# Linear attention and a token mixer on one core: PSUM tiles, transposes of x, the denominators' constant and the order of all steps are changed

## The chip, the core and the metric

The kernel runs on one core of one Trainium2 chip. The time is device microseconds, lower is better. A core has five engines with queues of their own that run side by side and in order: PE (TensorE, products of matrices; its loads of weights overlap with its products), DVE (VectorE), ACT (ScalarE), POOL (GpSimd) and SP (SyncE, which issues the transfers here). PE writes to PSUM, which has eight banks of 2 KB in each of 128 partitions; DVE and ACT read it from there, POOL works in SBUF.

## The reference, cut to what matters

Inputs are q, k and v of shape (8 batches, 8 heads, 576 positions, 64), and three weights. The attention has no softmax:

```
phi(x)  = [relu(x) * cos(theta * pos), relu(x) * sin(theta * pos)]     # 128 features
kv      = sum over positions of phi(k) outer v                         # 128 x 64 per head
z       = sum over positions of phi(k)
num     = phi(q) @ kv
den     = phi(q) @ z + 1e-06
x       = num / den, heads side by side                                # (8, 576, 512)
```

The mixer then works on x of each batch, with d_hyper = 64:

```
W     = (x @ w_q) @ (x @ w_k).T / 8
out   = relu(W @ x) @ w_out                                            # (8, 576, 512) float32
```

## The kernel before, in words

Loads and stores are float32, all products are in bfloat16 with float32 sums. The work is cut into half batches H = 0 to 15 (four heads each) and batches b = 0 to 7. A string, `ORDER`, lists some 500 steps; the program goes through it and issues each step's instructions, so on every engine's queue the instructions stand in that order. `KE3@A` is step KE of H = 3 on ACT (`@V` DVE, `@G` POOL); the digit behind a colon is a PSUM tile, or for OE one of ten output buffers. What the steps do, with their lines:

- `LQ`, `LK`, `LV` (line 130): SP loads q, k or v of H, in two transfers, into one of four raw buffers; the fifth load waits until the first buffer was read. `LW` loads the weights.
- `RQ`, `RK` (198 to 202), `CV`: relu or cast of a raw buffer to bfloat16, on POOL or ACT, into one of two buffers.
- `VS` (208): DVE multiplies v by the cosine and sine tables. The tables' two spare columns make the sums z come along as a 65th column.
- `KV` (221): 36 products give kv and z. `KE` (234) copies them to SBUF.
- `QT` (230): 18 transposes of 64 rows bring q's positions to the free axis. `QM` (238) multiplies them by the tables on DVE, for both halves of the features.
- `N` (254), one for each half of H's heads, g = 0 to 31: 20 products give numerators and, in the 65th column, denominators for ten groups of positions. Two small products (260) of a tile of ones and a tile `eps_t` add 1e-06 to the denominators in PSUM; `eps_t` holds the constant as the sum of two bfloat16 numbers, in two rows.
- `X` (268, 269): DVE takes the reciprocal of ten denominators per partition and multiplies the numerators by it, into x.
- `XT` (285): ten transposes of 128 by 128 turn x of H round, `XE` copies the result to xT (helper lines 189 on ACT, 193 on DVE).
- `WK` (302), `WQ` (315), `KX` (328): x @ w_k, x @ w_q, and the product of the first with x, which takes the place of the large matrix W. `KW`, `QW`, `XK` copy their results to SBUF.
- `MX` (339), `ME` (350, 352): the mixed rows, i = 0 to 31, and their scaled relu.
- `WO` (359), `OE`, `ST` (369): the last product for 36 tiles of 128 rows, its copy to one of ten output buffers, and SP's store.

PSUM is cut into five tiles. `PQ` (two banks) is used by QT and KV alone, each in a part of its own. Two tiles of two banks take N, XT and MX in turn, as the digits 1 and 2 in `ORDER` say. Two tiles of one bank (3 and 4) take WK, WQ, KX and WO. A product into a tile waits until what was in it has been read.

SP's queue holds the loads and the stores in the order of the list: a store that waits for its OE holds up the loads behind it.

Of the kernel before, what the change touches and what calls it, by code (L numbers as in the profile page):

```python
# [12 lines left out]
FP32 = mybir.dt.float32  # L13
# [6 lines left out]
EPS_HI = 9.9837780e-07  # L20
# [4 lines left out]
LQ0 LQ1 TB0 RQ0@G QT0 RQ1@G LV0 LV1 LK0 QM0 LW0 CV1@G LK1 CV0@A LV2 LQ2 VS0 RQ2@G QT1 LV3 QM1  # L25
RK0@A KV0 LK2 RK1@A VS1 CV3@G LQ3 LK3 KE0@V LW1 N1:1 X1 CV2@A LQ4 KV1 VS2 KE1@A N0:2 X0 CW0@A
N2:1 LV4 RK2@G LV5 RK3@G X2 QT2 QM2 XT0:2 LK4 N3:1 RQ4@G X3 XE0@A CV4@G KV2 KE2@A LQ5 LK5 N4:2
VS3 XT1:1 RQ3@A QT3 XE1@A CW1@A KV3 N5:1 X4 QM3 LW2 KE3@A LV6 RK4@G WK0:30 KW0@A WQ0:40 LQ6 N7:2
X5 QT4 N6:1 X7 KX0:30 XT2:2 X6 XK0@A XT3:1 XE2@A VS4 KV4 CV5@G LK6 LQ7 QW0@A MX2:2 LV7 XE3@V
ME2@A MX3:1 LK7 ME3@A LV8 WQ1:30 MX0:2 WK1:40 ME0@A KE4@V MX1:1 LQ8 QW1@A QM4 N8:2 ME1@A RQ5@G  # L30
QT5 KW1@A VS5 RK5@G N9:1 CW5@A KV5 X8 CW3@A X9 CW2@A LK8 CW4@A KX1:30 XK1@A XT4:2 XE4@A KE5@V
LV9 WO1:40 WO2:30 QM5 N11:2 OE1:0@A LQ9 CV6@G VS6 OE2:1@A N10:1 WO3:40 RQ6@G X11 QT6 RK6@A LK9
X10 LV10 RQ7@G MX7:2 LQ11 ME7@A OE3:2@A WO0:30 QM6 XT5:1 XE5@V MX5:2 ME5@V QT7 OE0:3@A KV6 KE6@A
WQ2:40 N12:1 CV7@G VS7 QW2@A MX4:2 ME4@A WK2:30 RK7@G LK11 LQ10 CV8@G KV7 KW2@A X12 N13:2 QM7
RQ8@G ST0 MX6:1 KX2:30 ME6@A LK10 X13 WO5:40 KE7@A XK2@A VS8 WO4:30 N15:1 QT8 RK8@G N14:2 X15
OE5:4@A X14 OE4:5@A KV8 KE8@A LV11 WO6:40 RQ9@G OE6:6@A XT6:1 XT7:2 WO8:30 XE6@A QM8 MX8:1 ME8@A
XE7@V MX9:2 ME9@A WQ3:40 CV9@G ST2 VS9 QT9 N17:1 MX10:2 RK9@G KV9 CV10@G LQ12 LV12 OE8:7@A
ME10@A WK3:30 MX11:2 X17 QM9 N16:1 QW3@A WO7:40 KW3@A KE9@A KX3:30 X16 VS10 ME11@A RQ10@A N18:1
X18 LK12 N19:2 X19 ST1 QT10 XK3@A ST4 WO10:30 LQ13 OE7:8@A WO12:40 RQ11@G OE12:9@A ST3 QM10
XT9:1 XT8:2 XE8@V RK10@G KV10 XE9@A CV11@G QT11 QM11 MX15:1 OE10:3@A RK11@G CV12@G MX12:2 WQ4:40  # L40
QW4@A WK4:30 WO11:40 RK12@G LK13 ME15@A ME12@V KW4@A VS11 VS12 MX13:2 RQ13@G MX14:1 KE10@A
ME13@A KX4:30 KV11 RQ12@A ME14@A XK4@A N21:2 OE11:1@A ST11 QT12 N20:1 KE11@A WO13:30 X21 X20
OE13:0@A LV13 KV12 ST7 LQ14 MX16:2 ME16@A N22:1 QM12 WO14:40 WO16:30 OE14:5@A ST14 LV15 X22
RK13@G KE12@A OE16:2@A N23:2 X23 QT13 MX19:1 ST5 WO9:40 ME19@A OE9:1@A QM13 XT11:2 XE11@A CV13@G
LV14 XT10:1 XE10@V WO17:30 OE17:8@A WO15:40 N25:2 LQ15 MX17:1 ME17@A VS13 RQ14@G X25 KV13 WK5:30
KE13@A N27:1 MX18:2 ME18@A OE15:5@V WQ5:40 ST6 QT14 X27 QW5@A ST16 KW5@A LK14 N24:2 X24 N26:1
X26 LK15 CV15@G QM14 WO21:40 KX5:30 RQ15@A ST15 XT13:2 XK5@A OE21:4@A XE13@V ST17 XT12:1 WO20:30
CV14@G XE12@A VS14 RK14@G ST13 OE20:6@V WO18:40 MX20:2 ME20@V ST9 MX23:1 ME23@A KV14 WQ6:30
KE14@A N28:1 QW6@A ST10 QT15 VS15 MX22:2 ME22@A RK15@G ST20 X28 WK6:30 KV15 KW6@A QM15 KE15@V
MX21:2 N29:1 OE18:2@A KX6:30 ME21@A X29 WO25:40 OE25:5@V N31:2 XK6@A X31 N30:1 X30 WO23:30  # L50
OE23:8@A ST23 WO24:40 XT14:2 XT15:1 OE24:0@A XE15@V ST18 WO22:40 XE14@A ST25 MX25:2 MX24:1
ME24@V WK7:30 OE22:1@A ME25@A KW7@A WQ7:40 QW7@V MX26:1 MX27:2 ME27@V WO26:30 OE26:3@A ME26@V
KX7:40 XK7@V ST12 WO27:30 OE27:6@A ST26 ST8 MX28:2 ME28@A MX31:1 ST22 ME31@V WO30:40 OE30:8@A
MX29:1 MX30:2 WO29:30 OE29:2@A ME29@V ST21 ST30 WO19:40 ST27 ST29 OE19:5@A ST19 WO28:30 OE28:9@A
ME30@V ST24 ST28 WO34:40 OE34:3@A ST34 WO35:30 OE35:7@A WO31:40 ST35 OE31:1@A ST31 WO32:30
OE32:4@V ST32 WO33:40 OE33:8@A ST33
# [4 lines left out]
def kernel(  # L61
# [15 lines left out]
    P = 128  # L77
# [38 lines left out]
    PQ = psum.tile([P, 2, 2048], U8, name="ps_qk")  # L116
    PT = [PQ] + [psum.tile([P, 2, 2048], U8, name=f"ps_p{i}") for i in range(2)]
# [27 lines left out]
    ones_t = pool.tile([P, P], BF16, name="ones")  # L145
    eps_t = pool.tile([P, SC], BF16, name="eps")
# [7 lines left out]
    def tables():  # L154
# [15 lines left out]
        nc.gpsimd.memset(ones_t, 1.0)  # L170
        nc.gpsimd.memset(eps_t, 0.0)
        for p in (0, H2):
            nc.gpsimd.memset(eps_t[p:p + 1, :], EPS_HI)
            nc.gpsimd.memset(eps_t[p + 32:p + 33, :], 1.0e-6 - EPS_HI)
# [37 lines left out]

    qt_v = PQ[:, :, 0:2 * S].bitcast(BF16)
    kv_v = PQ[:, :, 2 * S:2 * S + 4 * 2 * (D + 1)].bitcast(FP32)

    def KV(H, ps, eng):
        for c in range(C):
            for pr, r in ((0, 0), (1, 1), (1, 0), (0, 1)):
                a = slice(H2 * r, H2 * r + H2)
                o = slice(H2 * pr, H2 * pr + H2)  # L220
                nc.tensor.matmul(  # L221
                    kv_v[o, r, :], rk_b[H % NPREP][a, pr, c, :],
                    v2_b[H % NV2][a, pr, c, :, 0:D + 1],
                    start=(c == 0), stop=(c == C - 1))
# [209 lines left out]
```

## Time and profile before

| | |
|---|---|
| median of 3 runs | 126.11 us (125.97 to 126.49) |
| profiled execution | 127.19 us |
| its span, first to last instruction | 125.1 us |
| granted clock of PE over the span | 0.995 |
| PE busy | 102.2 us (82%), 2200 products |
| DVE busy | 92.4 us (74%), 123 instructions |
| ACT busy | 74.8 us (60%), 120 instructions |
| POOL busy | 55.2 us (44%), 59 instructions |
| read from and written to HBM | 29.62 MB and 9.44 MB, 312 GB/s over the span |

The span leaves out what lies before the first and behind the last instruction. Busy time is the time in which an engine had an instruction in work; on PE the ends are modelled, so a busy PE is not a PE at its peak, and overlapping instructions make durations longer than the distance from one start to the next. The view of 40 slices gives the busy share of an engine in tenths, a digit for 3.1 us. In the view of waits a line names the engine that waited, what it waited for, the total in us, how often, and the longest. In a timeline each line has the start in us, the duration in us, engine, line, operation and shapes.

### The profile page before, as it was taken

What the parts mean: (1) busy time and instruction counts of PE and PEld (TensorE: products, weight loads), DVE (VectorE), ACT (ScalarE), POOL (GpSimd) and SP (SyncE); (2) the same over time, 40 slices, a digit from 0 to 9 for tenths busy, and PEclk for the clock granted to TensorE, in tenths of its full rate; (3) what the DMA queues carried; (4) which work ended last, traced back from release to release, by engine and by line L of the source; (5) the groups of instructions that cost most, each with busy time, mean ns of one, the idle gap of its engine ahead of it and who ended that gap; (6) DMA issues with size and microseconds to landing.
All of it is one profiled execution on the core that took longest, in us unless ns stands there. A gap on an engine that the chain in (4) does not pass through costs nothing.

```text
span 125.1 us, 5077 instructions
## 1 busy us (share of the span) xinstructions
PE 102.2 (82%) x2200; PEld 66.7 (53%) x2200; DVE 92.4 (74%) x123; ACT 74.8 (60%) x120; POOL 55.2 (44%) x59
## 2 busy tenths in 40 slices
PE   0120768899696999899997999999997999999980
PEld 0110656787564556657654756575752756643430
DVE  1049598748996999899898698989698879576020
ACT  7523643443688784665874779686637673926640
POOL 7736067364947398696397263034332700000000
PEclk9999999999999999999999999999999999999998
DMA  4999999999999999999999910799999700808994
GB/s 113 337 383 374 391 397 367 378 391 390 387 393 390 391 389 390 389 378 396 398 399 399 362 56 0 194 303 375 392 403 387 279 19 0 335 34 313 371 375 170
DMA packets 20613, 39.38 MB, mean 315 GB/s; under 512 B 3184, under 2 KB 3184, under 8 KB 20592
## 3 DMA queue, kind: packets, MB, share of 16 engines
q1 hardware_dynamic: 20592, 39.07, 85.0%
q8 instruction: 17, 0.28, 0.9%
q14 instruction: 4, 0.03, 0.1%
HBM read 29.62 MB, written 9.44 MB: 312 GB/s over the span
## 4 chain that ended last, share of the span: by engine, by line
PE 57%; DMA 20%; DVE 6%; issue 4%; SPq 4%; POOL 3%; ACT 3%; POOLq 0%; ACTq 0%
PE ps_s L359 19%; DMA kraw<-in_k_dram 10%; PE ps_qk L221 8%; PE ps_p L254 7%; PE ps_s L328 6%; DMA out_dram<-o 5%; PE ps_p L285 5%; DMA qraw<-in_q_dram 5%; PE ps_s L302 4%; SPq L130 3%; PE ps_p L339 3%; PE ps_s L315 3%; PE ps_qk L230 3%; DVE x L269 3%; POOL rk L185 2%
## 5 line engine op out<-in xcount | busy, mean ns | idle before, releaser
L359 PE MATMUL ps_s<-wow,mix 128*128 128x512 bf16 x144 | 34.8, 380 | 0.7 <-ACT kx L189 0.7
L238 DVE TENSOR_TENSOR qm<-ps_qk,qtab 128x2304 bf16<-128x2304 bf16 x16 | 21.6, 1352 | 8.5 <-PE ps_qk L230 5.3
L269 DVE TENSOR_TENSOR x<-ps_p,rec 128x640 bf16<-128x640 f32 x32 | 26.4, 824 | 1.1
L189 ACT COPY o<-ps_s 128x512 f32<-128x512 f32 x32 | 18.7, 588 | 13.8 <-PE ps_s L359 13.5
L208 DVE TENSOR_TENSOR v<-vb,vtab 128x2304 bf16<-128x2304 bf16 x16 | 23.6, 1483 | 1.8 <-ACT vb L189 1.8
L185 POOL TENSOR_SCALAR rk<-kraw 128x1152 bf16<-128x1152 f32 x13 | 18.8, 1444 | 13.9 <-DMA kraw<-in_k_dram 7.9
L191 POOL TENSOR_SCALAR vb<-vraw 128x1152 bf16<-128x1152 f32 x14 | 17.3, 1239 | 14.0 <-DMA vraw<-in_v_dram 7.2
L185 POOL TENSOR_SCALAR rq<-qraw 128x1152 bf16<-128x1152 f32 x12 | 15.7, 1308 | 15.6 <-DMA qraw<-in_q_dram 12.1
L359 PEld LDWEIGHTS <-mix 128*128 128x128 bf16 x144 | 12.8, 98 | 14.7 <-issue 1.5
L254 PE MATMUL ps_p<-kvs,qm 64*128 64x65 bf16 x640 | 16.5, 200 | 3.2 <-issue 2.1
L350 ACT ACTIVATE mix<-ps_p 128x576 bf16<-128x576 f32 x23 | 14.7, 652 | 6.1 <-PE ps_p L339 6.0
L221 PE MATMUL ps_qk<-v,rk 64*64 64x130 bf16 x576 | 13.4, 242 | 5.6 <-ACT rk L183 4.0
L254 PEld LDWEIGHTS <-qm 64*128 64x128 bf16 x640 | 13.6, 100 | 8.0 <-issue 7.6
L230 PE MATMUL ps_qk<-ident,rq 64*128 64x64 bf16 x288 | 8.0, 202 | 9.0 <-POOL rq L185 8.6
L221 PEld LDWEIGHTS <-rk 64*64 64x64 bf16 x576 | 10.6, 120 | 7.9 <-ACT rk L183 4.1
L189 ACT COPY xT<-ps_p 128x1280 bf16<-128x1280 bf16 x9 | 11.0, 1227 | 4.5 <-PE ps_p L285 4.5
L285 PE MATMUL ps_p<-ident,x 128*128 128x128 bf16 x160 | 11.8, 231 | 0.4 <-issue 0.4
L285 PEld LDWEIGHTS <-x 128*128 128x128 bf16 x160 | 10.3, 103 | 2.8 <-DVE x L269 0.9
L230 PEld LDWEIGHTS <-rq 64*128 64x128 bf16 x288 | 6.1, 101 | 10.8 <-POOL rq L185 8.9
L268 DVE RECIPROCAL rec<-ps_p 128x10 f32<-128x10 f32 x32 | 6.9, 215 | 6.3 <-PE ps_p L260 5.8
L328 PE MATMUL ps_s<-x,wk 128*128 128x512 bf16 x40 | 10.0, 381 | 0.0
L189 ACT CAST kvs<-ps_qk 128x260 bf16<-128x260 f32 x12 | 4.6, 384 | 6.9 <-PE ps_qk L221 4.4
(44 smaller groups left out, 96.0 us busy)
## 6 DMA issues: line engine op xcount, KB each, us to landing
qraw<-in_q_dram SPq DMA_DIRECT2D x32, 288.0 KB, 6.0
vraw<-in_v_dram SPq DMA_DIRECT2D x32, 288.0 KB, 5.9
kraw<-in_k_dram SPq DMA_DIRECT2D x32, 288.0 KB, 6.0
out_dram<-o SPq DMA_DIRECT2D x36, 256.0 KB, 2.7
wof<-in_moe_w_out_dram SPq DMA_DIRECT2D x1, 1024.0 KB, 8.1
wqf<-in_moe_w_q_dram SPq DMA_DIRECT2D x1, 128.0 KB, 6.3
wkf<-in_moe_w_k_dram SPq DMA_DIRECT2D x1, 128.0 KB, 6.7
```

The costliest lines, as they stand in the source:

```text
L185: eng.tensor_scalar(dst, s, FMAX, 0.0, op0=ALU.min, op1=ALU.max)
L189: A.copy(dst, s)
L191: G.tensor_scalar(dst, s, 1.0, 1.0, op0=ALU.mult, op1=ALU.mult)
L208: V.tensor_mul(v2_b[H % NV2][:, :, :, :, 0:D], vb_b[H % NPREP].unsqueeze(3).to_broadcast([P, 2, C, 2, D]), vtab.unsqueeze(1).to_broadcast( ...
L221: nc.tensor.matmul(kv_v[o, r, :], rk_b[H % NPREP][a, pr, c, :], v2_b[H % NV2][a, pr, c, :, 0:D + 1], start=(c == 0), stop=(c == C - 1))
L230: nc.tensor.transpose(qt_v[:, r, c * H2:(c + 1) * H2], rq_b[H % NPREP][a, c, :, :], ident[a, a])
L238: V.tensor_mul(qm_b[H % NQM][:, :, :, 0:C, :].rearrange("p s r c d -> p s r (c d)"), qt_v.unsqueeze(1).to_broadcast([P, 2, 2, S]), qtab.re ...
L254: nc.tensor.matmul(nv[:, pr, u, :], qm_b[H % NQM][a, s, r, 2 * u:2 * u + 2, :], kv_b[H % 2][a, r, s, 0:D + 1], start=(u == 0 and s == 0), ...
L269: V.tensor_tensor(x_b[b % NX][:, :, 4 * h:4 * h + 4, :].rearrange("p u (w r) d -> p r w u d", r=2)[:, r], nv[:, :, :, 0:D], rec.to_broadca ...
L285: nc.tensor.transpose(o[:, w, u * P:(u + 1) * P], x_b[b % NX][:, u, hd:hd + 2, :], ident)
L328: nc.tensor.matmul(o, wk_b[b % 2][:, u, :, :], x_b[b % NX][:, u, :, :], start=(u == 0), stop=(u == SC - 1))
L359: nc.tensor.matmul(o, mix_b[bp % 2][:, m, rt * P:(rt + 1) * P], wow[:, m, :], start=(m == 0), stop=(m == NDM - 1))
```

## The change

Five things are changed together.

- PSUM: `PQ` is gone. There are three tiles of two banks, 0, 1 and 2, and QT and KV take whichever of them the list names, as N, XT and MX do.
- The constant: the products of `ones_t` and `eps_t` and both tiles with their memsets are gone. X starts with an instruction on DVE that adds 1e-06 to the ten denominators and writes them to SBUF; the reciprocal then works on that buffer in place.
- XT: twenty transposes of 64 rows instead of ten of 128, the two halves of the positions into one bank each. XE reads both banks and writes xT in the layout it had.
- Engines: on DVE 3 of the XE (before 7), 6 of the ME (9), 2 of the KE (4), no XK (1) and 8 of the OE (4); the others of these are on ACT. POOL has 13 RQ, 14 RK and 15 CV (before 12, 13 and 14).
- Order: the whole list is new. The first loads were q0, q1, v0, v1, k0 and are now q0, v0, k0, v1, k1, q1. Stores stand behind other loads.

```diff
-EPS_HI = 9.9837780e-07
...
-LQ0 LQ1 TB0 RQ0@G QT0 RQ1@G LV0 LV1 LK0 QM0 LW0 CV1@G LK1 CV0@A LV2 LQ2 VS0 RQ2@G QT1 LV3 QM1
-RK0@A KV0 LK2 RK1@A VS1 CV3@G LQ3 LK3 KE0@V LW1 N1:1 X1 CV2@A LQ4 KV1 VS2 KE1@A N0:2 X0 CW0@A
...
-QW4@A WK4:30 WO11:40 RK12@G LK13 ME15@A ME12@V KW4@A VS11 VS12 MX13:2 RQ13@G MX14:1 KE10@A
-ME13@A KX4:30 KV11 RQ12@A ME14@A XK4@A N21:2 OE11:1@A ST11 QT12 N20:1 KE11@A WO13:30 X21 X20
...
-ME30@V ST24 ST28 WO34:40 OE34:3@A ST34 WO35:30 OE35:7@A WO31:40 ST35 OE31:1@A ST31 WO32:30
-OE32:4@V ST32 WO33:40 OE33:8@A ST33
+LQ0 LV0 TB0 RQ0@G QT0:2 QM0 CV0@G LK0 RK0@A VS0 KV0:2 KE0@A N0:0 N1:1 LV1 LK1 RK1@A CV1@G VS1
+LQ1 RQ1@G LV2 LQ2 X1 X0 KV1:2 KE1@A CV2@G LK2 RK2@G RQ2@A QT1:2 QM1 N2:2 QT2:1 XT0:0 VS2 QM2 LQ3
+RQ3@G LV3 X2 CV3@G LK3 RK3@G XE0@A LW1 N3:0 LV5 LQ4 RQ4@G LK4 KV2:1 KE2@A QT3:2 N5:1 X3 XT1:0
...
+ME5@A RK7@G N13:2 KV7:1 KW2@A KX2:40 LQ8 OE2:2@A KE7@A XK2@A RQ7@G QT7:1 LQ9 CV8@G LK8 RQ9@G LV9
...
+OE11:6@V KW4@A CV12@G KV11:1 KE11@A WQ4:30 QW4@A N22:0 X22 N23:2 MX15:1 LV13 KX4:40 CV13@G ST11
...
+WQ5:30 N26:0 ST10 ST15 QW5@A VS14 XT12:1 N27:2 OE16:4@A X26 XE12@A ST0 WO18:30 WO20:40 OE20:8@A
+LQ15 RQ14@G QT14:0 MX22:1 OE18:9@A ST18 X27 XT13:2 XE13@V KV14:0 WO21:40 ME22@A WO9:30 OE21:7@A
...
+ST26 KE15@A N31:1 N30:2 XK6@A MX24:0 ME24@A X31 WO19:30 OE19:4@A WO24:40 OE24:0@A WO25:30 XT14:0
+XE14@A X30 XT15:1 OE25:3@V ST25 ST21 ST13 ST8 ST19 MX26:2 WO22:40 XE15@V MX25:1 MX27:0 OE22:9@V
+ME25@A ME27@V WQ7:30 QW7@A WK7:40 WO23:30 KW7@A KX7:40 OE23:3@A ST22 ST20 ST9 ST24 ST17 ST23
+ME26@V WO29:30 OE29:7@V XK7@A MX31:1 MX29:0 MX30:2 WO27:40 WO30:30 ME31@V MX28:1 ME30@V OE27:6@A
+ME29@A OE30:5@V ST30 ST29 ST27 ME28@A WO28:40 OE28:4@A ST28 WO35:30 OE35:9@A WO34:40 ST35
+OE34:8@A ST34 WO31:30 WO33:40 OE31:1@A ST31 OE33:0@V ST33 WO32:30 OE32:2@A ST32
...
 
...
     mix_b = bufs(2, [P, NDM, 2 * S], BF16, "mix")
     o_b = bufs(NOUT, [P, DM], FP32, "o")
 
-    PQ = psum.tile([P, 2, 2048], U8, name="ps_qk")
-    PT = [PQ] + [psum.tile([P, 2, 2048], U8, name=f"ps_p{i}") for i in range(2)]
+    PT = [psum.tile([P, 2, 2048], U8, name=f"ps_p{i}") for i in range(3)]
     PT += [psum.tile([P, 2048], U8, name=f"ps_s{i}") for i in range(2)]
     place = {}
 
...
     vtab = pool.tile([P, C, 2, D], BF16, name="vtab")
     qtab = pool.tile([P, 2, C, H2], BF16, name="qtab")
     ident = pool.tile([P, P], BF16, name="ident")
-    ones_t = pool.tile([P, P], BF16, name="ones")
-    eps_t = pool.tile([P, SC], BF16, name="eps")
     wq_f = pool.tile([P, NDM, DH], FP32, name="wqf")
     wk_f = pool.tile([P, NDM, DH], FP32, name="wkf")
     wo_f = pool.tile([P, NDM, DM], FP32, name="wof")
...
                 nc.scalar.activation(b[:, pr, :, :, D:DV],
                                      ki.unsqueeze(3).to_broadcast([P, C, 2, 2]),
                                      AF.Sin, bias=0.0, scale=coef)
-        nc.gpsimd.memset(ones_t, 1.0)
-        nc.gpsimd.memset(eps_t, 0.0)
-        for p in (0, H2):
-            nc.gpsimd.memset(eps_t[p:p + 1, :], EPS_HI)
-            nc.gpsimd.memset(eps_t[p + 32:p + 33, :], 1.0e-6 - EPS_HI)
         for b in qm_b:
             nc.gpsimd.memset(b[:, :, :, C, :], 0.0)
 
...
             vb_b[H % NPREP].unsqueeze(3).to_broadcast([P, 2, C, 2, D]),
             vtab.unsqueeze(1).to_broadcast([P, 2, C, 2, D]))
 
-    qt_v = PQ[:, :, 0:2 * S].bitcast(BF16)
-    kv_v = PQ[:, :, 2 * S:2 * S + 4 * 2 * (D + 1)].bitcast(FP32)
+    def qt_view(H):
+        return PT[place["QK", H]][:, :, 0:2 * S].bitcast(BF16)
+
+    def kv_view(H):
+        return PT[place["QK", H]][:, :, 2 * S:2 * S + 4 * 2 * (D + 1)].bitcast(FP32)
 
     def KV(H, ps, eng):
+        place["QK", H] = ps[0]
+        kv_v = kv_view(H)
         for c in range(C):
             for pr, r in ((0, 0), (1, 1), (1, 0), (0, 1)):
                 a = slice(H2 * r, H2 * r + H2)
...
                     start=(c == 0), stop=(c == C - 1))
 
     def QT(H, ps, eng):
+        place["QK", H] = ps[0]
+        qt_v = qt_view(H)
         for c in range(C):
             for r in range(2):
                 a = slice(H2 * r, H2 * r + H2)
...
 
     def KE(H, ps, eng):
         cast(eng, kv_b[H % 2][:, :, :, 0:D + 1],
-             kv_v.rearrange("p r (s e) -> p r s e", s=2))
+             kv_view(H).rearrange("p r (s e) -> p r s e", s=2))
 
     def QM(H, ps, eng):
         V.tensor_mul(
             qm_b[H % NQM][:, :, :, 0:C, :].rearrange("p s r c d -> p s r (c d)"),
-            qt_v.unsqueeze(1).to_broadcast([P, 2, 2, S]),
+            qt_view(H).unsqueeze(1).to_broadcast([P, 2, 2, S]),
             qtab.rearrange("p s c d -> p s (c d)").unsqueeze(2).to_broadcast([P, 2, 2, S]))
 
     def num(t):
...
                     nc.tensor.matmul(
                         nv[:, pr, u, :], qm_b[H % NQM][a, s, r, 2 * u:2 * u + 2, :],
                         kv_b[H % 2][a, r, s, 0:D + 1],
-                        start=(u == 0 and s == 0), stop=False)
-        for pr in range(2):
-            a = slice(H2 * pr, H2 * pr + H2)
-            nc.tensor.matmul(nv[:, pr, :, D], ones_t[a, :], eps_t[a, :],
-                             start=False, stop=True)
+                        start=(u == 0 and s == 0), stop=(u == SC - 1 and s == 1))
 
     def X(g, ps, eng):
         H, r = divmod(g, 2)
         b, h = divmod(H, 2)
         rec = rec_b[g % 3]
         nv = num(place["N", g])
-        V.reciprocal(rec, nv[:, :, :, D:D + 1])
+        V.tensor_scalar_add(rec, nv[:, :, :, D:D + 1], 1.0e-6)
+        V.reciprocal(rec, rec)
         V.tensor_tensor(
             x_b[b % NX][:, :, 4 * h:4 * h + 4, :].rearrange(
                 "p u (w r) d -> p r w u d", r=2)[:, r],
             nv[:, :, :, 0:D], rec.to_broadcast([P, 2, SC, D]), op=ALU.mult)
 
     def xt_view(i):
-        return PT[i].rearrange("p t e -> p (t e)").bitcast(BF16)[:, 0:2 * SC * P].rearrange(
-            "p (w n) -> p w n", w=2)
+        return PT[i].bitcast(BF16)[:, :, 0:2 * SC * H2].rearrange(
+            "p t (w u d) -> p t w u d", w=2, u=SC)
 
     def XT(H, ps, eng):
         b, h = divmod(H, 2)
         place["XT", H] = ps[0]
         o = xt_view(ps[0])
-        for w in range(2):
-            for u in range(SC):
-                hd = 4 * h + 2 * w
-                nc.tensor.transpose(o[:, w, u * P:(u + 1) * P], x_b[b % NX][:, u, hd:hd + 2, :],
-                                    ident)
+        for u in range(SC):
+            for w in range(2):
+                for t in range(2):
+                    a = slice(H2 * t, H2 * t + H2)
+                    hd = 4 * h + 2 * w
+                    nc.tensor.transpose(o[:, t, w, u, :], x_b[b % NX][a, u, hd:hd + 2, :],
+                                        ident[a, a])
 
     def XE(H, ps, eng):
         b, h = divmod(H, 2)
-        dst = xT_b[b % NXT][:, 2 * h:2 * h + 2].rearrange("p w c d -> p w (c d)")
-        cast(eng, dst, xt_view(place["XT", H]))
+        dst = xT_b[b % NXT][:, 2 * h:2 * h + 2].rearrange("p w (u t) d -> p w t u d", t=2)
+        cast(eng, dst, xt_view(place["XT", H]).rearrange("p t w u d -> p w t u d"))
 
     def bank(ps):
         t = PT[ps[0]]
```

## The prediction

> **What bounds the kernel now.** I read the page's busy shares first, then the row of slices, the chain that ended last, the waits, and the DVE and PE timelines. No engine is full: PE 82%, DVE 74%, ACT 60%. The slices and the chain are these.
>
> ```profile
> PE   0120768899696999899997999999997999999980
> DVE  1049598748996999899898698989698879576020
> DMA  4999999999999999999999910799999700808994
> ...
> PE 57%; DMA 20%; DVE 6%; issue 4%; SPq 4%; POOL 3%; ACT 3%; POOLq 0%; ACTq 0%
> ```
>
> PE and DVE are both high in nearly every slice from 15 to 106 us; the DMA engines have a hole at 71 to 78 us and one near 100. The chain is mostly PE, so PE looks like the bound. The waits say that it is a pair:
>
> ```profile
> DVE rec L268 <- PE ps_p L260: 5.8, 11, 0.9
> DVE qm L238 <- PE ps_qk L230: 5.3, 2, 5.1
> DVE qm L238 <- PE ps_qk L221: 2.0, 2, 1.8
> DVE xT L193 <- PE ps_p L285: 2.0, 3, 1.0
> SPq L369 <- ACT o L189: 17.1, 11, 8.9
> ```
>
> DVE waits for products of PE in short pieces; SP stood up to 8.9 us at a store whose rows ACT had not written (that is the first hole). DVE's timeline gives the price of an instruction, as the distance from start to start of neighbours that wait for nothing:
>
> ```profile
> 44.35 0.21 DVE L268 RECIPROCAL rec<-ps_p 128x10 f32<-128x10 f32 x1
> 44.59 0.82 DVE L269 TENSOR_TENSOR x<-ps_p,rec 128x640 bf16<-128x640 f32 x1
> 45.33 0.21 DVE L268 RECIPROCAL rec<-ps_p 128x10 f32<-128x10 f32 x1
> 45.58 0.82 DVE L269 TENSOR_TENSOR x<-ps_p,rec 128x640 bf16<-128x640 f32 x1
> 46.32 1.35 DVE L238 TENSOR_TENSOR qm<-ps_qk,qtab 128x2304 bf16<-128x2304 bf16 x1
> 47.58 0.81 DVE L193 COPY xT<-ps_p 128x1280 bf16<-128x1280 bf16 x1
> ```
>
> The division of 10 sums holds the engine 0.245 us, the product behind it 0.74, a QM 1.27, an XE 0.73. Read in the same way: VS 1.27, ME on DVE 0.68, OE 0.61, KE 0.34; on ACT XE 1.14, ME 0.56, OE 0.50, KE 0.30, a relu or cast of a raw buffer 1.07. On PE the timeline gives these:
>
> ```profile
> 57.81 1.28 PE L285 MATMUL ps_p<-ident,x 128*128 128x128 bf16 x20
> 58.93 1.03 PE L359 MATMUL ps_s<-wow,mix 128*128 128x512 bf16 x4
> ...
> 60.97 0.44 PE L230 MATMUL ps_qk<-ident,rq 64*128 64x64 bf16 x18
> 61.24 0.47 PE L254 MATMUL ps_p<-kvs,qm 64*128 64x65 bf16 x20
> 61.55 0.17 PE L260 MATMUL ps_p<-eps,ones 64*128 64x5 bf16 x2
> 61.58 0.28 PE L339 MATMUL ps_p<-wq,kx 64*128 64x288 bf16 x2
> ```
>
> Twenty 128-row transposes (two XT) take 1.12 us, 18 transposes of 64 rows (a QT) 0.27, the pair with the constant 0.03. A WO takes 0.88 (32 matmuls in 7.04 at the end), KV 0.65, N without the pair 0.30, KX 1.09, WK 0.69, WQ 0.61, MX 0.17. The rest goes by its group's mean less 0.1 (ACT), or as it stands (POOL: q 1.31, k 1.44, v 1.24).
>
> **The change part by part.**
>
> Constant on PE removed: 32 pairs by 0.03 is 1.0 us of PE. Six small memsets on POOL (3.09 to 3.95 us) go too; POOL's first relu of q starts at 4.50 behind them, but q0 was issued at 0.74 and the quickest q load took 2.9 us, so at most 0.8 us is to be had; I take 0.
>
> Constant on DVE added: 32 adds of 10 elements from PSUM, each read by the reciprocal behind it. The row nearest is the reciprocal, also 10 elements from PSUM and also read by the next: 0.245 us each, 7.8 us in all. The reciprocal now reads SBUF and waits for the add; no row shows that. Low end: 0.14 us, what the chain counts for a reciprocal, 4.5 us in all. High end: 0.26, 8.3. I take 7.8. [...]
>
> Transposes: 20 of 64 rows at QT's rate are 0.30 us; with some switching I put 0.35 against 0.56, so 16 XT save 3.4 us of PE. If the halves didn't overlap, nothing; at QT's rate exactly, 4.2. XE reads the same 1280 elements, in runs of 64 from two banks: ACT at the same price; DVE at the same (3 of them), at worst double, 2.2 us more.
>
> PSUM tiles: QT and KV leave their own tile and share three with N, XT and MX: 112 uses over three, where it was 80 over two and 32 over one. PE work between two uses of a tile has a median of 1.8 us now and 1.7 before; in 20 cases of 109 it is shorter than the reader's own time, before in 22. I take no gain and no loss; a bound either way is the wait of DVE for ps_qk named above, 2 us.
>
> Order and engines. DVE gives away four XE, three ME, two KE and one XK, and takes four OE: 3.9 us less, so with the adds 4.0 more. ACT gets four XE, three ME, two KE, one XK, loses four OE and three raw casts: 2.1 more; the three casts go to POOL, 4.0 more. PE has 4.3 less.
>
> To see where these fall I added the prices along each order's list, engine by engine, in four stages of eight X steps (DVE, PE, ACT, POOL, us). Before: 18.5 10.7 10.1 13.3; 22.2 19.4 16.0 14.5; 21.6 23.4 18.2 16.1; 19.9 19.7 12.1 7.9. After: 20.1 7.5 7.2 15.8; 22.4 21.4 22.9 17.4; 21.8 21.0 15.2 14.7; 21.8 22.6 16.1 8.0. What is left for PE behind the last X: 17.1 before, 13.5 after. So the saving on PE turns up behind the last X, where DVE is idle, and up to it PE has nearly the same (72.5 against 73.2), DVE 3.9 more, ACT 4.9 more.
>
> Start. Loads land 1.5 us apart (casts start at 6.99, 8.49, 10.06, 11.59). With the new order v0 is the second, k0 the third: k0 at 8.5 and not 11.6. From there: RK0 to 9.6, KV0 (1.19 in these early microseconds) to 10.8, KE0, N0 and N1 to 12.6, X1 and X0 to 15.1. But q1 is now the sixth load: 13.1, so QM1 ends at 16.4, VS2 17.7, QM2 19.3, X2 20.5. At 20.5 DVE then has 74.7 us listed up to its last X; before, at 20.9, 71.2. The early start is given back to the late q1.
>
> PE runs at half pace until 28.3 us (the 20 products of an N last 0.73 before and 0.48 after it), though the granted clock reads 0.9 or more. [...] PE may warm some microseconds sooner or later; DVE leads there, so I put 0, bounds 1 us either way.
>
> Middle. Before, DVE took from 20.9 to 106.1 for 71.2 us of work, so 13.9 were waits. With the same waits the last X ends at 20.5 + 74.7 + 13.9 = 109.1, 3.0 later.
>
> Loads. Eleven stores stand ahead of the last load in both orders. SP will stop at ST11 as it did, until DVE writes those rows (59.9 on its list, about 78 us), with LK13, LQ13 and LK14 behind it; KV13 is some 12 us later. LQ15, behind ST15 (about 92 us), lands by 95 to 98, QM15 needs it near 102. Hidden, with 4 us to spare. On POOL, RQ9 stands ahead of RK8 now and waits for QT7 to give its buffer back, with RK8 and CV9 queued behind; KV8 stands 8 us of DVE's list behind QT7, and POOL is listed for 56 us in 100: hidden. The weights' loads stay among the first third.
>
> End. Behind the last X: XT15, then XE15 on DVE behind an OE, done at 1.4; MX26, WO22, MX25, MX27, WQ7, WK7 to 3.1; KW7 on ACT with WO23 beside it to 4.0; KX7 5.1; XK7 5.75 beside WO29, 6.0; three MX, WO27, WO30, MX28, WO28 to 9.3; five WO to 13.7; copy 14.4; store and close 2.9, as before (122.2 to 125.1). That is 17.3, with a little slack 17.5; before, 19.0. So 1.5 earlier.
>
> Sum: 3.0 less 1.5 is 1.5 by equal waits. The stages give the same by another way: the largest engine of each stage adds up to 84.0 before and 87.4 after, 3.4 less 1.5 is 1.9. I take 1.7. The profiled execution took 127.19 with a span of 125.1, so it would become 128.9; it stood 1.1 above the median of 126.11, so the median becomes 127.8.
>
> **The rivals.** First, PE is the bound after all: for it the chain's 57%, and PE idle only 5 of the 75 us from 30 to 105; against it, that PE's busy time counts latencies (its list has 63 us there) and that the work up to the last X hardly shrinks. It decides if DVE's adds fit into its 13.9 us of waits. Then PE's 4.0 and 1.0 come off in full: 121.1, faster. [...] Third, no change: half the adds fall into waits and the shorter end pays for the rest, 126.1. Fourth, coupling gets worse: in the second stage ACT has 22.9 beside DVE 22.4 and PE 21.4, and in stages of four X the largest engines sum to 91.0 against 84.6: 6.4 less 1.5, 131.0; with slow XE copies on DVE 133.
>
> **How the numbers follow.** Forecast 0.40, PE the bound 0.22, cheap add 0.08, no change 0.12 (a tenth within 0.5%, the rest split), worse coupling 0.18. Half a per cent, 0.63 us, is about what a measurement of this kernel tells from nothing. So faster 0.31, same 0.10, slower 0.59. Range: 121.0 (PE the bound) to 133.0 (worse coupling with slow copies). The slower cases' own range is 126.8 to 133.0.
>
> **What would show it.** A group of 32 adds with starts 0.245 us ahead of their reciprocals; DVE's last X near 109 us and busier, its waits near 14 us; XT's 20 transposes in 0.3 to 0.35; under 18 us from the last X to the end; k0's relu at 8.5 and q1's at 13.1; ACT full between the eighth and sixteenth X. The forecast is wrong if the reciprocal on SBUF starts within 0.15 us of its add, if DVE's waits fall below 10 us, or if LQ15 lands after QM15 could run.

## The result, and the profile after

The changed kernel took 131.99 us (median of 4 runs, 130.9 to 132.29) where the kernel before took 126.3 beside it (median of 4, 125.97 to 128.65): the ratio is 1.0444 [1.0363 to 1.0525], slower. The forecast was 127.8. The sign was right, the time lies inside the range and 4.2 us above the point. The profiled execution of the changed kernel took 130.9, 3.7 us more than that of the kernel before (127.19; the span is 129.1 for 125.1), where the sum had 1.7. Of the other 2.2 us of the miss, half is that the profiled execution before stood 1.1 above its median and half that this one stands 1.1 below its own. On the chips of the later experiments the kernel before had medians of 128.05 to 128.16, so kernels of different chips are compared here by their ratios. A ratio with an interval leaves out slow runs, those over 1.5% above the fastest of their kernel; where only one run of four is left, the medians of all runs are compared without an interval, and such a figure is loose by 1 to 3%.

The page of the changed kernel: busy shares, four rows of the 40 slices, and the engines' shares of the chain that ended last.

```profile
PE 100.7 (78%) x2296; PEld 61.9 (48%) x2296; DVE 95.6 (74%) x149; ACT 76.8 (59%) x123; POOL 56.4 (44%) x56
...
PE   0208459599877799989966699997799999999960
...
DVE  1085997679999688999969628999698999747120
...
PEclk9999999999999999999999779999999999999997
DMA  4999999999999999999999000999995702299693
...
PE 46%; DMA 32%; DVE 8%; issue 6%; SPq 2%; ACT 2%; DVEq 0%
```

PE is busy 1.5 us less than before (100.7 against 102.2), DVE 3.2 more (95.6 against 92.4), and neither is full. Two things are new. PE has slices of 6 and 7 in the middle, and in two slices, 71 to 77 us, the granted clock drops to 7. The chain has fewer per cent of PE (46 for 57) and more of loads and of "issue", time in which the engine waited for nothing that the profile shows. The waits, as engine, line and tile, what was waited for, then us in total, how often, and the longest:

```profile
DVE qm L236 <- PE ps_p L228: 11.2, 5, 5.1
...
ACT xT L180 <- PE ps_p L282: 9.5, 7, 2.9
...
PE ps_p L282 <- issue: 3.9, 2, 2.3
...
PE ps_p L217 <- issue: 1.8, 2, 1.6
...
PE ps_s L356 <- issue: 1.0, 1, 1.0
```

DVE still waits for PE, now in longer pieces (a QM for QT, 11.2 us in five). PE itself pauses: 3.9 us in two pauses in the middle of an XT (line 282), 1.8 in two within a KV, 1.0 within a WO. These pauses are what the experiments had to explain.

The adds, in DVE's timeline (start, us, engine, line and operation):

```profile
13.67 0.16 DVE L262 TENSOR_SCALAR rec<-ps_p 128x10 f32<-128x10 f32 x1
13.87 0.22 DVE L263 RECIPROCAL rec<-rec 128x10 f32<-128x10 f32 x1
14.12 0.82 DVE L264 TENSOR_TENSOR x<-ps_p,rec 128x640 bf16<-128x640 f32 x1
14.97 1.36 DVE L236 TENSOR_TENSOR qm<-ps_p,qtab 128x2304 bf16<-128x2304 bf16 x1
```

From start to start an add holds DVE 0.195 us in the mean of 32 (0.19 to 0.20); the reciprocal, now from SBUF, 0.25, as before from PSUM. And PE at its longest pause, with the idle time before a row and its releaser in brackets:

```profile
69.24 0.44 PE L228 MATMUL ps_p<-ident,rq 64*128 64x64 bf16 x18
69.51 0.29 PE L336 MATMUL ps_p<-wq,kx 64*128 64x288 bf16 x2
69.72 0.26 PE L282 MATMUL ps_p<-ident,x 64*128 64x64 bf16 x5
72.25 0.40 PE L282 MATMUL ps_p<-ident,x 64*128 64x64 bf16 x15 [2.27 <-issue]
72.58 3.59 PE L356 MATMUL ps_s<-wow,mix 128*128 128x512 bf16 x8
```

Five transposes of an XT run, then PE stands for 2.27 us, though the profile shows nothing that the other fifteen wait for, and the eight products of two WO behind it take 3.59 us where the same eight take 1.9 elsewhere: the clock has fallen. The windows of one microsecond there (span of the window, busy us and instructions of PE, PEld, DVE, ACT and POOL, granted clock, share of the DMA engines, GB/s) show both:

```profile
69.00:70.00 1.00, 0.98 (x49) 0.63 (x37) 0.94 (x2) 0.83 (x2) 0.53 (x1) 1.00 1.05 404
70.00:71.00 1.00, 0.00 (x0) 0.00 (x0) 1.00 (x2) 0.00 (x0) 0.92 (x2) 1.00 0.69 263
71.00:72.00 1.00, 0.00 (x0) 0.00 (x0) 1.00 (x3) 0.00 (x0) 0.85 (x1) 1.00 0.19 67
72.00:73.00 1.00, 0.75 (x17) 0.43 (x18) 1.00 (x1) 0.31 (x1) 0.00 (x0) 0.81 0.08 32
73.00:74.00 1.00, 1.00 (x4) 0.43 (x3) 0.05 (x1) 1.00 (x2) 0.36 (x1) 0.50 0.06 16
```

**Where the pauses stand.** I counted PE's products from the start up to each pause of 0.2 us or more that is put down to "issue". Every one, before and after, stands behind product 95, 223, 351, 479 and so on, in steps of 128; only the late mark 1759 shows as 1758, which fits if instructions of PE that only wait count too: by then two of them have passed before, three after. Each product comes with one weight load (2200 and 2200 before, 2296 and 2296 after), so the step is 256 instructions of PE's list, whatever line happens to stand there. Such a place is called a mark below, and the 256 instructions up to the next a block.

| kernel | behind product: pause, us | sum | span |
|---|---|---|---|
| before | 479: 0.40, 607: 1.23, 863: 0.39, 1247: 0.85, 1758: 0.20 | 3.1 | 125.1 |
| after | 351: 0.21, 607: 0.76, 735: 1.67, 1247: 0.98, 1375: 2.27, 1758: 1.59 | 7.5 | 129.1 |

So 4.4 us more of pauses, and 1.7 (3.59 less 1.9) of WO at a low clock, partly covered by other work, against a span that grew by 4.0. The page's queue of kind "instruction" fits: 17 packets and 0.28 MB for the 2200 products before, 18 and 0.29 MB for the 2296 after, that is some 16 KB a packet, and two instructions for each of 2200 products are 17.2 blocks of 256.

The traces also list every packet of the transfers with its start and duration, and they show what a pause waits for. There are as many 16 KB packets of that queue as PE passes marks, 17 and 18. In all eleven pauses of the table PE starts again 1.23 to 1.53 us after the end of such a packet: the pause of 2.27 us ends at 72.25, behind a packet of 69.70 to 70.78. The packet for the next block starts only behind the mark ahead of it. At the 24 marks of both traces at which the DMA engines were full (95 to 1247, 1631 and 1758) it started 2.4 to 4.0 us behind the mark and took 0.9 to 1.2 us; at 1375 and 1503, in the hole of the transfers, it started within 1.6 us. So PE pauses where it runs through a block sooner than the packet with the next one has come. That short instructions, such as the 64-row transposes, make this more likely is an estimate from the 3.70 and 3.93 us in which the blocks ahead of the pauses of 1.67 and 2.27 us were run through.

### The profile page after: what moved, and what is told of

The parts are those of the page before. It is cut to its first block, busy times and chain, and to the rows that moved or that the text cites. A ratio compares the mean times of both kernels' runs of the same rounds, so it can differ in the third digit from the quotient of the medians.

```text
span 129.1 us, 5294 instructions
## 1 busy us (share of the span) xinstructions
PE 100.7 (78%) x2296; PEld 61.9 (48%) x2296; DVE 95.6 (74%) x149; ACT 76.8 (59%) x123; POOL 56.4 (44%) x56
## 4 chain that ended last, share of the span: by engine, by line
PE 46%; DMA 32%; DVE 8%; issue 6%; SPq 2%; ACT 2%; DVEq 0%
PE ps_s L356 21%; DMA kraw<-in_k_dram 14%; DMA vraw<-in_v_dram 10%; DMA qraw<-in_q_dram 8%; PE ps_s L325 5%; PE ps_p L252 4%; PE ps_p L217 4%; PE ps_p L336 3%; PE ps_p L282 3%; PE ps_s L299 3%; DVE v L199 2%; SPq L128 2%; DVE qm L236 2%; PE ps_s L312 2%; PE ps_p L228 2%
## 5 line engine op out<-in xcount | busy, mean ns | idle before, releaser
L236 DVE TENSOR_TENSOR qm<-ps_p,qtab 128x2304 bf16<-128x2304 bf16 x16 | 21.7, 1354 | 12.9 <-PE ps_p L228 11.2
L180 ACT COPY o<-ps_s 128x512 f32<-128x512 f32 x28 | 16.4, 589 | 11.7 <-PE ps_s L356 9.4
L180 ACT COPY xT<-ps_p 128x1280 bf16<-128x1280 bf16 x13 | 16.0, 1228 | 9.7 <-PE ps_p L282 9.5
L347 ACT ACTIVATE mix<-ps_p 128x576 bf16<-128x576 f32 x26 | 16.7, 654 | 4.5 <-PE ps_p L336 3.4
L217 PE MATMUL ps_p<-v,rk 64*64 64x130 bf16 x576 | 13.9, 242 | 6.8 <-ACT rk L174 3.2
L228 PE MATMUL ps_p<-ident,rq 64*128 64x64 bf16 x288 | 7.9, 202 | 6.3 <-POOL rq L176 5.7
L282 PE MATMUL ps_p<-ident,x 64*128 64x64 bf16 x320 | 8.2, 197 | 4.5 <-issue 3.9
L180 ACT CAST kvs<-ps_p 128x260 bf16<-128x260 f32 x14 | 5.3, 379 | 9.8 <-PE ps_p L217 5.3
L184 DVE COPY o<-ps_s 128x512 f32<-128x512 f32 x8 | 5.5, 688 | 7.6 <-PE ps_s L356 7.6
L282 PEld LDWEIGHTS <-x 64*128 64x128 bf16 x320 | 6.2, 99 | 6.9 <-issue 5.0
```

The lines of the kernel that those rows point to most:

```text
L180: A.copy(dst, s)
L217: nc.tensor.matmul(kv_v[o, r, :], rk_b[H % NPREP][a, pr, c, :], v2_b[H % NV2][a, pr, c, :, 0:D + 1], start=(c == 0), stop=(c == C - 1))
L228: nc.tensor.transpose(qt_v[:, r, c * H2:(c + 1) * H2], rq_b[H % NPREP][a, c, :, :], ident[a, a])
L236: V.tensor_mul(qm_b[H % NQM][:, :, :, 0:C, :].rearrange("p s r c d -> p s r (c d)"), qt_view(H).unsqueeze(1).to_broadcast([P, 2, 2, S]), q ...
L282: nc.tensor.transpose(o[:, t, w, u, :], x_b[b % NX][a, u, hd:hd + 2, :], ident[a, a])
L347: A.activation(dst, s, AF.Relu, scale=scale_moe)
```

## The experiments

Three explanations were weighed. *Supply*: PE pauses at every 256th instruction, and 320 more instructions for XT with 64 fewer for the constant make it worse. *DVE*: the pauses are incidental and the 32 adds are the cost. *Order*: the new order or the three shared PSUM tiles cost the time, by ACT or by waits for tiles. The first four kernels undo or add the two small parts one at a time; the intervals are 95%, and where none is given only the medians stand against each other. "Before" beside these four had 128.05 (13 runs).

**Ten 128-row transposes in the changed kernel.**

```diff
-        for u in range(SC):
-            for w in range(2):
-                for t in range(2): ... nc.tensor.transpose(o[:, t, w, u, :], x_b[..][a, u, hd:hd + 2, :], ident[a, a])
+        for w in range(2):
+            for u in range(SC): ... nc.tensor.transpose(o[:, w, u * P:(u + 1) * P], x_b[..][:, u, hd:hd + 2, :], ident)
```

> The changed kernel with one part undone: x is turned by ten 128-row transposes, as before. 320 PE instructions fewer than the changed kernel (4274 against 4594 in its list), but 3.4 us more of listed PE time. Theory A, instruction supply: in both traces PE stops with nothing to wait for (releaser 'issue') only at product 95, 223, 351 and so on, every 128 products, that is every 256 instructions, and while the DMA engines are full no such block of 256 passes in less than 5.4 to 6.2 us. 320 fewer are 1.25 blocks: the pauses, 7.5 us in the changed kernel, fall to 3 or less, the clock does not drop at 70 to 76 us, and the median falls from 132.0 to 126 to 129. Theory B, the sums of the prediction (DVE and the order lengthen the way to the last X, PE's saving is real): no better, 132 to 134.5.

Measured: 128.4 us (11 runs), 1.0033 [0.9988 to 1.0078] of before, against the changed kernel's 1.0444: 4% faster, though PE now has 3.4 us more work by the list. Nearly the whole loss is gone. Less PE work was not less time. The other signs of theory A are not borne out by the one trace, which is of the longest of the eleven runs (133.45): its pauses at marks sum to 5.0 us, not 3 or less, and the clock drops at 51 and 92 us (four products of a KX take 1.91 us there, for 1.03). Nor is the limit in the text above quite right: the shortest block with full DMA engines took 5.1 us, before, from 50.97 to 56.07.

**64-row transposes in the kernel before** (the same edit the other way).

> The kernel before with one part of the change: x turned by twenty 64-row transposes, two banks, XE reading both. 320 PE instructions more (4722). Theory A, instruction supply: more and longer pauses at the 256-instruction marks (3.1 us before, 6 to 9 now); 128 to 132. Theory B, listed time: PE has 3.4 us less work beside an unchanged DVE, so 123 to 126.3.

Measured: 130.77 us (4 runs), 1.0229 [1.0151 to 1.0308]. The transposes do get cheaper, their products are busy 7.1 us where it was 11.8, and yet the kernel is slower. (PE's total falls from 102.2 to 98.9, but that trace lacks the records of 18 products of WO and KX, so the total says little.) PE's timeline of this kernel at two of its pauses:

```profile
56.32 1.89 PE L361 MATMUL ps_s<-wow,mix 128*128 128x512 bf16 x8 [1.30 <-issue]
...
60.78 0.44 PE L287 MATMUL ps_p<-ident,x 64*128 64x64 bf16 x18
61.97 0.50 PE L287 MATMUL ps_p<-ident,x 64*128 64x64 bf16 x22 [0.75 <-issue]
```

The first stands between a KX and two WO, the second within a pair of XT; behind it the 22 transposes run at their usual rate. Its pauses of 0.2 us or more sum to 8.6 us in a span of 129.7 (before 3.1 in 125.1), with no fall of the clock (its mean over the span is 1.0).

**The changed kernel without the adds.**

```diff
-        V.tensor_scalar_add(rec, nv[:, :, :, D:D + 1], 1.0e-6)
-        V.reciprocal(rec, rec)
+        V.reciprocal(rec, nv[:, :, :, D:D + 1])
...
-            nc.gpsimd.memset(b[:, :, :, C, :], 0.0)
+            nc.gpsimd.memset(b[:, :, :, C, :], 1.0)
```

> The changed kernel without the constant: the 32 adds on DVE are left out and the reciprocal reads PSUM (the padding columns of qm are set to 1 so that no denominator is zero). This leaves 1e-06 out of the computation and gives the padding rows values. PE instructions are unchanged (4594). Theory A, supply: PE's pauses stay near 7 us, and the 32 x 0.195 = 6.2 us taken from DVE come off only where DVE leads: 129 to 132. Theory B, DVE as the bound: most of 6.2 us comes off, 126 to 128.5.

Measured: 129.67 us (4 runs, 127.42 to 131.09, no interval), 1.013 of before by the medians. Taking out 32 adds, 6.2 us at 0.195, is worth some 3% or 3.9 us by these medians; as the four runs lie apart, anything from 2 to 6 us fits. The pauses did not go: those at marks sum to 8.2.

**The kernel before with the constant on DVE** (no small products, one add ahead of each reciprocal).

> The kernel before with one part of the change: the constant added on DVE, the 64 small products on PE gone. 128 PE instructions fewer (4274), 6.2 us more on DVE (32 adds at the 0.195 us that the changed kernel's trace shows from an add's start to its reciprocal's). Theory A, supply: half a block fewer, pauses at most 2 us, which pays for part of the adds: 125 to 128. Theory B, DVE as the bound with its waits kept: 129.5 to 132.

Measured: 134.61 us (4 runs, 131.4 to 140.13, no interval), 1.05 by the medians, or 6.6 us: as much as the adds are long (6.2), and above the 3.9 that taking them out of the changed kernel gave. PE's list is shorter by the 64 small products, which also moves every mark by up to 64 products. The pauses sum to 4.9 us, where theory A had 2 at most: one of 3.78 us stands within the 20 products of an N, and the KX and XT behind it run slowly (2.23 us for 1.24, 2.00 for 1.28). Whether leaving out products can cost too is what the next kernels ask. "Before" beside them had 128.1 (19 runs).

**The new order and the three tiles alone**: 128-row transposes, and the constant back on PE.

```diff
+        for pr in range(2):
+            a = slice(H2 * pr, H2 * pr + H2)
+            nc.tensor.matmul(nv[:, pr, :, D], ones_t[a, :], eps_t[a, :], start=False, stop=True)
...
-        V.tensor_scalar_add(rec, nv[:, :, :, D:D + 1], 1.0e-6)
-        V.reciprocal(rec, rec)
+        V.reciprocal(rec, nv[:, :, :, D:D + 1])
```

> The changed kernel with both small parts undone: ten 128-row transposes, and the constant added by the 64 small products on PE. What is left of the change is the three interchangeable PSUM tiles with the new order and its engines. On this chip the kernel before took 128.05 in the last comparison, with 128-row transposes alone undone the changed kernel was level with it. If the new order is worth what the prediction's list says (DVE 6.2 us less than with the adds, PE 1 us more, the rest as it was): 1 to 4% below the kernel before. If the order is no better than the old one: level, within 1%. If it is worse in itself: over 1% slower.

Measured: 126.11 us (10 runs), 0.9841 [0.9787 to 0.9894]: faster than before, by 1.1 to 2.1%. It is the fastest version here that computes the reference. The order with its engines and the tiles are the good part of the change: the prediction booked 3.9 us less of DVE's work for the engines, part of the 1.5 us at the end, and nothing for the tiles; 2.0 us came. The order and the tiles were not tried apart.

**Both small parts under the old order.**

> The kernel before, its order and PSUM tiles, with both small parts of the change: 64-row transposes and the constant added on DVE. If the two costs found one by one add up (2.3% and 3 to 5%): 1.05 to 1.08. If both are paid out of the same waits: 1.03 to 1.05, and then the new order with its PSUM tiles costs nothing. Instruction supply: 4594 PE rows, as in the changed kernel, so pauses of 4 to 8 us at the 256-instruction marks.

Measured: 132.54 us (4 runs, 129.69 to 134.69, no interval), 1.035 by the medians. Under the old order the transposes cost 2.3%, the add 5%, both together 3.5%: by these medians they do not add. The pauses, expected at 4 to 8 us, sum to 3.4 in its trace. That what one part costs depends on where the other has moved the marks is a reading that fits, not one that this run shows.

**No constant anywhere in the kernel before**: the adding kernel above without its adds, and the padding set to 1.

> The kernel before without the constant: neither the 64 small products nor an add (1e-06 is left out of the computation; the padding columns of qm are set to 1). 128 PE instructions fewer, 1 us of listed PE time less, DVE unchanged. Against the kernel with the add on DVE it gives the price of 32 adds with nothing else changed. Instruction supply: half a block fewer, 1 to 3 us faster than before. Listed time alone: 0 to 1 us faster. The adds: 4 us or more between this kernel and the one with the add if DVE is on the path; under 2 us if they fall into waits.

Measured: 130.97 us (11 runs, 128.46 to 132.83), 1.0092 [1.0032 to 1.0152]. With 64 small products taken out and nothing put in, the kernel is slower, not faster. Against it, the kernel with the adds and the same list on PE stands 3.6 us higher by the medians: a second price for the 32 adds, beside 3.9 and as loose. PE in the profiled execution, the longest of the eleven:

```profile
90.70 0.78 PE L247 MATMUL ps_p<-kvs,qm 64*128 64x65 bf16 x39
94.75 0.21 PE L247 MATMUL ps_p<-kvs,qm 64*128 64x65 bf16 x1 [3.27 <-issue]
94.90 1.89 PE L348 MATMUL ps_s<-wow,mix 128*128 128x512 bf16 x4
96.58 2.34 PE L317 MATMUL ps_s<-x,wk 128*128 128x512 bf16 x5
```

The fortieth product of two N, behind product 1758, comes 3.27 us late, and four WO products then take 1.89 us, twice their price.

**64 idle products at the start of that kernel.** If the place of the marks is what matters, work that does nothing can give the time back.

```diff
         V.memset(warm, 1.0)
+        for _ in range(64):
+            nc.tensor.matmul(PT[4].bitcast(FP32)[:, 0:8], warm[:, 0:P], warm[:, 0:8], start=True, stop=True)
```

> The kernel before without the constant, as in the run without the small products, and with 64 idle products of 8 columns at the very start, while PE waits for the first q (their result is read by nobody). So work is added, in idle time, and the 128 instructions that were taken out are back in the list ahead of everything. The later 256-instruction marks then fall near where they fell in the kernel before. If the 3 us by which leaving out the small products made it slower come from where the marks fall (a pause of 3.3 us inside an N at product 1759, and half speed of PE behind it), this kernel is faster than the one without the idle products, at or below the kernel before: 0.98 to 1.00 of it. If they come from anything else (DVE, loads, chance), it stays at 1.005 to 1.02.

Measured, with "before" at 128.16 (7 runs) for this and the kernels below: 125.8 us (4 runs), 0.9872 [0.9765 to 0.998], from 1.0092 [1.0032 to 1.0152] without the idle products. More instructions, and 2.2% faster. The same place in its trace:

```profile
89.55 0.78 PE L247 MATMUL ps_p<-kvs,qm 64*128 64x65 bf16 x40
90.27 1.04 PE L348 MATMUL ps_s<-wow,mix 128*128 128x512 bf16 x4
91.14 1.24 PE L317 MATMUL ps_s<-x,wk 128*128 128x512 bf16 x5
```

The forty products run through, and WO and KX have their normal price. So the pause of 3.27 us was neither in the N nor in any tile or wait of it. That this pause makes the 2.2% is not shown: its trace is of the longest run, and no trace is of the five runs, 128.46 to 129.23, on which the ratio rests. The pauses that are left (0.35, 1.14, 1.07, 0.21) stand at marks again, now behind 991, 1247, 1375 and 2014.

**The same 64 idle products in the fastest kernel.**

> The fastest kernel so far (new order and PSUM tiles, 128-row transposes, constant on PE) with the same 64 idle products at the start, which move every mark half a block. Theory of the marks: its pauses, 4.2 us in all, at products 351, 479, 607 and 863, move 64 products earlier in the list and change their lengths; the time changes by up to 2% either way: 0.97 to 1.00 of the kernel before. Without an effect of the marks: 0.984 again, within 0.5%.

Measured: 131.82 us (4 runs), 1.0289 [1.0134 to 1.0445], from 0.9841 [0.9787 to 0.9894]: 4.6% slower by the very edit that made the other 2.2% faster. The idle products don't act by an earlier full clock: its records begin, at the full clock, at 25.4 us without them and 25.6 with them, and in the other kernel at 18.88 without and 28.95 with them. The pause, in its PE timeline:

```profile
62.58 0.60 PE L225 MATMUL ps_p<-v,rk 64*64 64x130 bf16 x26
65.74 0.36 PE L225 MATMUL ps_p<-v,rk 64*64 64x130 bf16 x10 [2.57 <-issue]
66.04 0.30 PE L345 MATMUL ps_p<-wq,kx 64*128 64x288 bf16 x2
66.27 2.04 PE L334 MATMUL ps_s<-x,wk 128*128 128x512 bf16 x5
```

It is a KV that is cut this time, behind product 1247, and KX behind it takes 2.04 us for 1.24.

**A test of what the blocks compete with**: the kernel before with 64-row transposes, q loaded for its first four steps only, 7 MB less to move.

```diff
         b, h = divmod(H, 2)
+        if nm == "q" and H >= NRAW:
+            return
```

> The kernel before with 64-row transposes, and q loaded for the first four half batches only (the later ones work on those four again, so the output is of other data): 7 MB fewer of 39 are moved, PE's instructions are the same 4722. If PE's pauses at the 256-instruction marks come from its instructions waiting among full DMA engines, they fall from some 8.6 us to under 4 us once the loads thin out (after some 25 us). If they come from PE's own rate of working alone, they stay at 7 us or more.

Measured: 128.59 us in one run ("before" beside it 128.1). Its pauses sum to 6.3 us, between what the two theories gave, and so this is inconclusive. The trace speaks for competition with transfers: the pauses of 0.5 us and more all end while the DMA engines are full (21, 28, 34, 56 and 63 us), and none of 0.2 us or more falls in the stretches where the missing loads leave them thin.

**The store of tile 11 moved.** In the fastest kernel ST11 goes behind LK14; the store then writes rows of a later product.

```diff
-... CV13@G ST11 LK13 RK13@G ... LK14 RK14@G ...
+... CV13@G LK13 RK13@G ... LK14 ST11 RK14@G ...
```

> The same fastest kernel with one store moved: ST11, at which SP stops for some 10 us while the DMA engines run empty, stands behind LK14 and not ahead of LK13, so three loads are issued early. The prediction called this stop hidden: then level with the same kernel with the store in its place, 0.984 within 0.5%. If the hole delays the last half batches: 0.965 to 0.975 of the kernel before.

Measured: 126.02 us (4 runs), 0.9859 [0.97 to 1.0018], level with 0.9841. So SP's stop at that store, 12 us in the changed kernel, is hidden, as far as an interval that wide can tell: it still holds 0.97.

**The constant back on PE, with 64-row transposes kept.**

> The changed kernel with the constant back on PE (64 small products) and 64-row transposes kept; 4722 PE rows, the longest list of all, 320 more than the kernel with 128-row transposes. If the costs of the two small parts under the new order are as found (128-row transposes gave 4.1%, the adds about 2%), and add up: 1.02 to 1.03 of the kernel before. If the transposes' cost comes from instruction supply and the longer list makes it worse: 1.03 to 1.05.

Measured: 131.66 us (4 runs, 128.38 to 132.28, no interval), 1.027 by the medians. It closes the square under the new order: with neither part 0.984, with the add 1.003, with the transposes 1.027, with both 1.044. There the add costs 1.7 to 1.9% and the transposes 4.1 to 4.3%, and with the 1.6% that the order and tiles gain the parts give the whole. The corner of 1.027 is loose: by its lowest run, 1.006, the transposes alone cost 2.2% and the add behind them 3.8. What holds with intervals is the other path, the add first (0.984 to 1.003), the transposes on top (1.003 to 1.044).

## Why the prediction was right in sign and short in size

**The sign** was right in part by luck. The prediction had the kernel slower because of the adds, with the transposes as a saving of 3.4 us of PE. Without the 64-row transposes the rest of the change is level (1.0033), so the part booked as a saving makes the loss.

**The start** was right: QM1 starts at 14.97 and X2 ends at 20.3 (forecast 20.5), and the early k0 is given back to the late q1. The 0 for the end of PE's half pace was right too: the records of the clock begin, at the full clock, at 28.39 us before and at 28.25 after. What ends the half pace no run shows. Not right was the granted clock of 0.9 or more beside it: ahead of these times the traces have no record of the clock, and the view puts full clock where none is.

**The add** ("the row nearest is the reciprocal ... I take 7.8"): the mechanism held, the term was mis-sized. An add takes 0.195 us and not 0.245, so 6.2 us were listed, and taking them out was worth 3.6 and 3.9 us by medians; with PE's small products in their place it was 1.9% under the new order, some 2.4 us. The reciprocal took 0.22 us from SBUF and 0.21 from PSUM before.

**The transposes** ("so 16 XT save 3.4 us of PE"): the price held, 0.29 to 0.40 us for twenty against the 0.35 taken, where no pause cuts them and behind the slow first microseconds; XE cost what it did. What failed is that the step counted PE's time and not PE's instructions. The 160 added products and their 160 weight loads are one and a quarter blocks of 256 more, where the traces have a packet of 16 KB for each mark passed (17 and 18), and every later mark falls elsewhere. This part is the loss: 2.3% under the old order, 4.1% under the new.

**The constant on PE** ("32 pairs by 0.03 is 1.0 us of PE"): taking the pairs out gained nothing that shows; alone it cost 0.9%. That it did so by moving the marks fits the 64 idle products, which made that kernel 2.2% faster.

**The middle** ("With the same waits the last X ends at 20.5 + 74.7 + 13.9 = 109.1"): it ended at 110.1. The list was 1.5 us shorter than put (29 adds behind X2, 0.05 less each, 73.2), the start 0.2 earlier, and the waits were 16.5, 2.6 more. The premise of equal waits is the step that fell. In the same stretch PE pauses 7.5 us, before 3.1; I had seen "issue" at 4% of the chain, and gave it no term.

**The end** ("17.5; before, 19.0"): it took 19.0. XE15 ended at 112.0, 2.0 behind the last X (1.4 forecast); KX7 began at 114.7 and ended at 115.8, 5.7 behind (5.1); the last WO ended at 124.64, 14.6 behind (13.7), and from the last copy's end at 125.27 to the close it was 3.8 us and not 2.9. So the gain of 1.5 did not come. Why the close was longer was not tried.

**Loads and SP** were right: SP stood from 67.5 to 79.9 at ST11, LQ15 was issued at 94.0 and QM15 began at 104.5, not waiting for it, and moving ST11 changed nothing.

**The rivals.** "PE is the bound after all" (its sum took 5.0 us off; PE's list is 4.3 shorter, which gives 121.8) is refuted in its consequence: kernels with less work on PE's list were slower (64-row transposes under both orders, no constant under the old one), and idle work made one faster. The cheap add (0.08) and "no change" fell. "Coupling gets worse", 131.0, came nearest in number, but its place was ACT in the second stage; what the runs showed in its stead is PE standing at marks of its own list. The test named for it, ACT full between the eighth and sixteenth X, doesn't carry the loss: 128-row transposes with the same ACT list bring the ratio to 1.0033.

**What is shown and what stays open.** Shown: the pauses stand at marks, 256 instructions of PE or a multiple of it apart, and end 1.2 to 1.6 us behind the packet of instructions for the next block; this holds for all 67 pauses of 0.2 us or more at marks in the traces of the fourteen kernels. (Four more, of 0.30 to 0.34 us, stand elsewhere, at half clock, ahead of a WO or KX in two traces that lack records of these.) Shown too: 64 idle products, which move the marks, are worth 2.2% one way and 4.6% the other. That packets come late because they share the DMA engines with the loads is read from where they come late, and from the lengths of blocks: with full DMA engines a block with its pause took 5.6 and 6.2 us before (4.72 + 0.85, 4.96 + 1.23) and 5.4 and 6.2 after (3.70 + 1.67, 3.93 + 2.27), while from 97.67 to 101.00, with the DMA engines at 0.50, a block ran in 3.33 without a pause. The one run meant to decide it was inconclusive. A pause also differs between runs of one list: in the fastest kernel they sum to 3.9 us, and with one store moved, PE's list being the same, to 1.5. Open too is how much of the transposes' 2.3 and 4.1% is their count and how much the place where the marks fell; a kernel with as many instructions and other marks would tell.

## What to carry to other kernels

Count the instructions of an engine as well as their time: an edit that halves the work of each and doubles their number can lose (here 2.3 and 4.1%), and a pause put down to "issue" should be counted from the start of the list, for here they stood 256 instructions or a multiple of it apart. Before believing a few per cent of a single edit in such a kernel, move the marks by idle instructions and see whether the verdict stays. Undo a compound change part by part: here the order and the PSUM tiles gained 1.6%, which the two small parts beside them turned into a loss of 4.4%.

## What the runs showed of the hardware

- PE paused up to 3.78 us (the kernel before with the constant on DVE) with nothing to wait for that the profile shows, at marks 256 instructions apart (behind product 95 + 128 n, the late ones one sooner), until 1.17 to 1.62 us after a 16 KB packet of the instruction queue had ended.
- With the DMA engines full that packet started 2.4 to 4.0 us behind the mark ahead of it, in a hole of the transfers within 1.6 us (both kernels).
- 64 idle products of 8 columns made one kernel 2.2% faster and another 4.6% slower.
- The granted clock fell to half behind the pauses of 2.27, 2.57, 3.27 and 3.78 us, not behind those of 2.20 and 2.21; behind shorter ones it fell in some places (1.75 and 1.65) and not in others (1.67 and 1.59 in the changed kernel). In the traces of both kernels it changes only 3.41 us or a multiple of it apart (after 44.37, 3.41 and 51.20 us in the changed kernel, after 95.57 before). Of the 3.41 us that ended with a fall PE had stood 0.67 in the changed kernel, by the 2.27 us (the fall came at 72.62, 2.6 us after PE had stopped), and 0.51 where the constant is back on PE with 64-row transposes, by the 1.75; without a fall it stood 0.43 in the changed kernel, by the 1.59, and under 0.4 in the kernel before without the constant, by the 2.21, of which 39.35 us, the end of such a stretch, cuts off a part.
- An add of 10 elements from PSUM to SBUF takes 0.195 us from start to start on DVE, a reciprocal of 10 elements 0.25 from either memory.
